# Scoring attention with unsplit float32 products of q and k, and theta with fp16 halves, in a fused attention and mixing kernel on one core

## The chip, the core and the metric

The kernel runs on one core of a Trainium2 chip. The metric is the device time of one execution in microseconds. Five engines work side by side, each through its own queue of instructions: PE (TensorE: PE is its matmuls, PEld its weight loads), DVE (VectorE), ACT (ScalarE), POOL (GpSimd) and SP, which here only issues transfers.

## The reference

Attention over 8 batches of 8 heads, 576 positions and 64 features, with a causal window of 128 and a linear bias, and then a mixing layer over the joined heads (512 channels):

```python
scores = scale * np.matmul(q, k.transpose(0, 1, 3, 2))
mask = (rel >= 0) & (rel < window)                      # window = 128
scores = np.where(mask, scores + bias[None], -1000000000.0)
attn = softmax(scores); attn_out = np.matmul(attn, v)
x = attn_out.transpose(0, 2, 1, 3).reshape(B, S, H * D)
theta = x @ w_theta
zr, zi = x * np.cos(theta), x * np.sin(theta)
y = np.einsum('ts,bsd->btd', w_tok_r, zr) + np.einsum('ts,bsd->btd', w_tok_i, zi)
u = x + y
return u + np.maximum(u @ w_ch, 0.0)
```

(softmax stands for the reference's maximum, exponential and normalization.) q, k and v are float32; the four weights of the mixing layer are float64.

## The kernel before

**Precision.** A product that must be better than one reduced pass is made of halves: an operand is split into a high part and the rest, and three products (high by high, rest by high, high by rest) are summed in PSUM. q and k, theta's x and w_theta, and u and w_ch are split into float32 halves of the type float32r; the weights P and v of the late heads, z and w_tok into fp16 halves.

**Stages.** Two heads form a pair `p`; 32 pairs, four to a batch.

- `load_pair` fetches q and k of a pair, transposed, each [128, 576] with one head on the upper 64 rows and the other on the lower. `split_pair` makes the halves: ACT casts qh (L395) and kh (L399), DVE subtracts ql (L396), and DVE (first eight pairs, two batches) or POOL (the others) subtracts kl (L329, a helper's line that also makes z_lo).
- `scores` goes through five tiles of up to 128 queries by 192 or 256 keys, in three groups ((0, 2), (3, 4), (1,)), all through one PSUM tile `s_ps` of two banks, a head in each. For each tile three products for two heads (L490). Then DVE adds the band (slope and mask) and takes the minimum (L506, two instructions each), and ACT takes the exponential (L511).
- The first seven pairs (`EARLY`) are turned on PE (L569) and multiplied by v in float32 (L579); the later ones are split into fp16 halves (ACT L525, DVE L527), turned by DMA and multiplied by v's halves (L597). DVE normalizes into `x_sb` (L542 to L546).
- `turn` is run once per batch: x is turned (PE L618), split (ACT L630, DVE L632) and copied (ACT L635), then theta for each of five row blocks (PE L650: 12 products of 512 columns, or 8 for the last 64 rows, which pack both halves of x into one operand). `w_theta` carries a factor 1/(2 pi), so the nearest integer is subtracted (ACT L664, DVE L665), and sine and cosine follow on ACT (L671, L673), z on DVE (L677) and its halves (ACT L682, L329).
- `mix` sums over positions (PE L713, 216 products of 288 columns a batch), `channels` over channels (PE L741, 96 products), and DVE adds (L719, L748).
- The float64 weights are unpacked into float32 on DVE and ACT (L338 to L376) at the start. For w_tok PE sums the magnitudes of columns (L348: products of ones with the exponents), and a power of two from their maximum (L780 to L790) scales the fp16 halves (L793, L796). w_theta's halves come straight from `whole` (L368, L370).

**Order.** Nothing is ordered by hand. `Plan` records every step with its buffers and a written cost, simulates the engines forward and backward six times, and emits the steps in the best order found. Where its plan leaves PE without work, `Plan.run` puts in fillers (`spin`, L297: products of ones into the unused end of an accumulator bank), which keep PE busy and compute nothing.

Of the kernel before, what the change touches and what calls it, by code (L numbers as in the profile page):

```python
# [13 lines left out]
F32 = mybir.dt.float32  # L14
# [84 lines left out]
class Step:  # L99
    __slots__ = ("n", "engine", "busy", "late", "emit", "deps", "after", "table", "port", "start")  # L100


class Plan:
# [5 lines left out]
    def add(self, engine, busy, late, emit, deps, table=None, port=False):  # L109
        s = Step()  # L110
        s.n, s.engine, s.emit, s.table, s.port = len(self.steps), engine, emit, table, port
        s.busy, s.late, s.deps, s.after = busy, late, deps, []
        for d in deps:
            self.steps[d].after.append(s.n)
        self.steps.append(s)
        return s

    def __call__(self, engine, cost, emit, r=(), w=(), table=None, port=None):
# [105 lines left out]
def attn_moe_kernel(ctx: ExitStack, tc: tile.TileContext, qt, kt, vx, wth, wtok, wch, band, out):  # L224
# [19 lines left out]
    peak, wscale, shrunk = fixed[:, 133:134], fixed[:, 134:135], fixed[:, 136:144]  # L244
    bands = place("bands", [128, H, 256], BF16)
    columns_at = [144]
# [9 lines left out]
    zs_ring = small(3, 3)  # L256
# [3 lines left out]
    wth_hi, wth_lo = place("wth_hi", [128, 4, DM], F32R), place("wth_lo", [128, 4, DM], F32R)  # L260
# [13 lines left out]
    qr_ring, kr_ring = ring("qr", 1, [128, S], F32), ring("kr", 1, [128, S], F32)  # L274
    qk_ring = Ring([tuple(place(n, [128, S], F32R) for n in ("qh", "ql", "kh", "kl"))])
# [10 lines left out]
    fg_ring = ring("fg", 2, [128, 2, 512], F32)  # L286
    xp_ring = ring("xp", 2, [128, 2, 512], F32R)
# [3 lines left out]
    spun = a_ring.tiles[1][:, NT * 65:]  # L291

    def spin(count):

        same = white.bitcast(BF16)
# [28 lines left out]
    held = [Buf(v) for v in values_at]  # L324

# [5 lines left out]
    def unpack(src, c, w, finish, last=False, first=False, summed=None, raw_buf=None):  # L331
# [13 lines left out]
        if summed:  # L345
            def add():
                for k in range(2):
                    nc.tensor.matmul(summed.tile[:, :HALF], white, ex.bitcast(F32)[:, k * HALF:(k + 1) * HALF],  # L348
# [10 lines left out]
    def whole(hi, lo, buf, scale):  # L359
        def finish(c, w, val, ex, E, M):  # L360
            plan("DVE", dve(w), lambda: nc.vector.tensor_tensor(out=val, in0=val, in1=ex, op=ALU.mult), r=[E], w=[M],
                 port=True)
            if scale is None:
                plan("ACT", act(w), lambda: nc.scalar.copy(hi[:, c, :], val), r=[M], w=[(buf, ("h", c))])
                less("POOL", w, lo[:, c, :], val, hi[:, c, :].bitcast(F32), r=[M, (buf, ("h", c))],
                     w=[(buf, ("l", c))])
            else:
                plan("ACT", act(w), lambda: nc.scalar.activation(hi[:, c, :], val, AF.Copy, scale=scale),  # L368
                     r=[M], w=[(buf, ("h", c))])
                plan("DVE", (0.61, 0.13), lambda: nc.vector.scalar_tensor_tensor(  # L370
                    out=lo[:, c, :], in0=val, scalar=scale, in1=hi[:, c, :].bitcast(F32), op0=ALU.mult,
                    op1=ALU.subtract), r=[M, (buf, ("h", c))], w=[(buf, ("l", c))], port=True)
        return finish

    def keep(c, w, val, ex, E, M):
        plan("DVE", dve(w), lambda: nc.vector.tensor_tensor(out=held[c].tile, in0=val, in1=ex, op=ALU.mult),  # L376
             r=[E, M], w=[(held[c], 0)], port=True)


    raw_qk, split_qk, group_v, group_scale = {}, {}, {}, {}  # L380
# [9 lines left out]

    def split_pair(p):
        qr, kr = raw_qk.pop(p)
        buf = qk_ring.take()
        qh, ql, kh, kl = buf.tile
        plan("ACT", act(S), lambda: nc.scalar.copy(qh, qr.tile), r=[(qr, 0)], w=[(buf, "qh")])  # L395
        plan("DVE", dve(S), lambda: nc.vector.tensor_tensor(  # L396
            out=ql, in0=qr.tile, in1=qh.bitcast(F32), op=ALU.subtract),
            r=[(qr, 0), (buf, "qh")], w=[(buf, "ql")], port=True)
        plan("ACT", act(S), lambda: nc.scalar.copy(kh, kr.tile), r=[(kr, 0)], w=[(buf, "kh")])  # L399
        less("POOL" if p >= QUICK * PAIRS_OF else "DVE", S, kl, kr.tile, kh.bitcast(F32),  # L400
             r=[(kr, 0), (buf, "kh")], w=[(buf, "kl")])
        split_qk[p] = buf
# [47 lines left out]
    def regain(b):  # L450
# [19 lines left out]
    def scores(p, weights):  # L470
        late = p >= EARLY
        qk = split_qk.pop(p)
        qh, ql, kh, kl = qk.tile
        terms = ((qh, kh), (ql, kh), (qh, kl))
        mx_buf = mx_ring.take()
        mx = mx_buf.tile.rearrange("p (e i) -> p e i", e=2)
        for tiles in GROUPS:
# [5 lines left out]
            def multiply(tiles=tiles, ps=ps, wide=wide):  # L483
                for k, i in enumerate(tiles):
                    q0, qn, k0, kn, _ = TILES[i]
                    kn = kn if wide else 256
                    for j, (qm, km) in enumerate(terms):
                        for e in range(2):
                            rows = slice(64 * e, 64 * e + 64)
                            nc.tensor.matmul(ps.tile[:qn, e, 256 * k:256 * k + kn], qm[rows, q0:q0 + qn],  # L490
                                             km[rows, k0:k0 + kn], start=(j == 0), stop=(j == 2))
            plan("PE", pe(360 * len(tiles) + 190), multiply, r=[(qk, x) for x in ("qh", "ql", "kh", "kl")],
                 w=[(ps, 0)])
# [109 lines left out]
    def turn(b, x_buf, zs):  # L603
        isx, ISX = zs.tile[:, 1:2], (zs, 1)
        xtf = xtf_ring.take()
# [3 lines left out]
        def columns(i):  # L609
# [12 lines left out]
            if i == 0:  # L622
                both = x_hi.rearrange("p (c a t) -> p c a t", a=2, t=64)
                plan("ACT", act(370), lambda: nc.scalar.activation(both[:, :, 0], src, AF.Copy, scale=isx),
                     r=[(x_ps, 0), ISX], w=[(xp, "h")])
                plan("DVE", (0.395, 0.13), lambda: nc.vector.scalar_tensor_tensor(
                    out=both[:, :, 1], in0=src, scalar=isx, in1=both[:, :, 0].bitcast(F32), op0=ALU.mult,
                    op1=ALU.subtract), r=[(x_ps, 0), (xp, "h"), ISX], w=[(xp, "l")])
            else:
                plan("ACT", act(600), lambda: nc.scalar.activation(x_hi, x_ps.tile, AF.Copy, scale=isx),  # L630
                     r=[(x_ps, 0), ISX], w=[(xp, "h")])
                plan("DVE", (0.66, 0.13), lambda: nc.vector.scalar_tensor_tensor(  # L632
                    out=x_lo, in0=x_ps.tile, scalar=isx, in1=x_hi.bitcast(F32), op0=ALU.mult, op1=ALU.subtract),
                    r=[(x_ps, 0), (xp, "h"), ISX], w=[(xp, "l")])
# [4 lines left out]
        def angle(i):  # L639
# [12 lines left out]
            plan("PE", pe(4 * len(prods) * (238 if i else 245)), multiply,  # L652
# [11 lines left out]
            plan("ACT", act(512), lambda: nc.scalar.activation(r[:n], th, AF.Copy, bias=MAGIC), r=[THK], w=[R])  # L664
# [215 lines left out]
```

## Time and profile before

| | |
|---|---|
| median of 3 runs | 688.94 us (686.01 to 689.36) |
| profiled execution | 687.63 us |
| its span, first to last instruction | 685.6 us |
| PE busy | 657.5 us (96%) |
| DVE, ACT, POOL busy | 576.1, 541.5, 198.7 us (84, 79, 29%) |
| fillers (L297) | 292, 33.3 us of PE |
| score products (L490) | 960 matmuls |
| theta products (L650) | 448 matmuls |

The span is the time from the first to the last instruction; the execution's own time is 2.0 us longer. Matmuls are pipelined and overlap in the trace, so the distance between the starts of two of them tells more than the length of one. Busy shares are averages over the whole span, and the stages differ: rows by stretch of time are needed beside them. A row of two or more instructions (x2) gives the time from the first start to the last end.

### The profile page before, as it was taken

To read this page: it belongs to the slowest core of one execution; us is meant where nothing else is said; L and a number is where in the kernel's file an instruction comes from. 1 tells how busy PE (TensorE), PEld (TensorE's weight loads), DVE (VectorE), ACT (ScalarE), POOL (GpSimd) and SP (SyncE) were. 2 spreads that over 40 slices of the span, in tenths; PEclk is the share of its full clock that TensorE was granted. 3 is DMA by queue.
4 is the path that set the end of the run, shared out by engine and by line. 5 is a ranking of instruction groups with operands and counts; after the bars stand their busy time and mean duration, and the time that the engine had idled before them with its cause. 6 is when DMAs were issued, how large, how long until landed. Compare 5 with 4: busy or idle time off the path is not lost.

```text
span 685.6 us, 15977 instructions
## 1 busy us (share of the span) xinstructions
PE 657.5 (96%) x6144; PEld 548.2 (80%) x6144; DVE 576.1 (84%) x1556; ACT 541.5 (79%) x975; POOL 198.7 (29%) x211
## 2 busy tenths in 40 slices
PE   7999988898999799999999999999999999999998
PEld 6787776786787677887788778987898879878877
DVE  7999999899899999999998988989979978636312
ACT  5866899946789989998999989888989998335310
POOL 0000002123411124633273335432623351315220
PEclk9999999999999999999999999999999999999999
DMA  9465212285756457657655774277465736000101
GB/s 335 161 194 178 66 35 74 59 187 131 133 116 139 123 108 162 139 141 143 144 121 141 138 165 88 80 176 151 100 130 116 122 59 115 27 1 27 44 1 70
DMA packets 147148, 79.52 MB, mean 116 GB/s; under 512 B 120192, under 2 KB 136576, under 8 KB 147072
## 3 DMA queue, kind: packets, MB, share of 16 engines
q1 hardware_dynamic: 147072, 78.50, 48.4%
q8 instruction: 48, 0.79, 0.5%
q14 instruction: 28, 0.23, 0.1%
HBM read 39.55 MB, written 9.44 MB: 71 GB/s over the span
## 4 chain that ended last, share of the span: by engine, by line
PE 40%; ACT 6%; DVE 3%; issue 1%; DVEq 0%; ACTq 0%
PE m_psb L713 9%; PE m_psa L713 8%; PE t_psb L650 7%; PE m_psb L741 5%; PE m_psa L741 4%; PE s_ps L490 3%; PE a_psb L597 1%; PE a_psa L597 1%; PE t_psa L650 1%; PE t_psa L618 1%; ACT L673 1%; DVE fgb L677 1%; ACT z_hi L682 1%; ACT L511 0%; ACT hlb L525 0%
## 5 line engine op out<-in xcount | busy, mean ns | idle before, releaser
L713 PEld LDWEIGHTS <-z_hi 128*128 128x128 f16 x1152 | 109.1, 99 | 36.5 <-issue 7.0
L713 PE MATMUL m_psb<-wtk_hi,z_hi 128*128 128x288 f16 x288 | 83.2, 289 | 2.9 <-DVE xtfa L719 2.5
L713 PE MATMUL m_psa<-wtk_hi,z_hi 128*128 128x288 f16 x288 | 83.3, 289 | 0.0
L713 PE MATMUL m_psa<-wtk_lo,z_hi 128*128 128x288 f16 x288 | 83.2, 289 | 0.0
L713 PE MATMUL m_psb<-wtk_hi,z_lo 128*128 128x288 f16 x288 | 83.1, 289 | 0.0
L713 PE MATMUL m_psa<-wtk_hi,z_lo 128*128 128x288 f16 x288 | 83.1, 289 | 0.0
L713 PE MATMUL m_psb<-wtk_lo,z_hi 128*128 128x288 f16 x288 | 83.0, 288 | 0.0
L713 PEld LDWEIGHTS <-z_lo 128*128 128x128 f16 x576 | 56.8, 99 | 15.1 <-DVE z_lo L329 0.3
L329 POOL TENSOR_TENSOR kl<-kra,kh 128x576 fp32r<-128x576 f32 x24 | 38.3, 1597 | 97.8 <-ACT kh L399 92.4
L490 PE MATMUL s_ps<-kh,qh 64*128 64x256 f32 (+1 forms) x320 | 53.4, 328 | 10.8 <-DVE fixed L506 9.9
L490 PEld LDWEIGHTS s_ps<-kh,qh 64*128 64x128 f32 (+1 forms) x320 | 28.6, 173 | 29.4 <-DVE fixed L506 13.2
L329 POOL TENSOR_TENSOR z_lo<-fgb,z_hi 128x512 f16<-128x512 f32 x27 | 35.7, 1337 | 42.6 <-ACT z_hi L682 22.9
L725 POOL TENSOR_TENSOR u_lo<-xtfb,u_hi 128x288 fp32r<-128x288 f32 x32 | 31.5, 994 | 56.4 <-ACT u_hi L723 54.5
L329 POOL TENSOR_TENSOR z_lo<-fga,z_hi 128x512 f16<-128x512 f32 x27 | 37.1, 1388 | 35.5 <-ACT z_hi L682 35.4
L490 PE MATMUL s_ps<-kh,ql 64*128 64x256 f32 (+1 forms) x320 | 44.7, 274 | 1.4 <-DVE ql L396 1.2
L725 POOL TENSOR_TENSOR u_lo<-xtfa,u_hi 128x288 fp32r<-128x288 f32 x32 | 30.3, 953 | 54.1 <-ACT u_hi L723 53.2
L490 PE MATMUL s_ps<-kl,qh 64*128 64x256 f32 (+1 forms) x320 | 44.4, 272 | 0.5 <-POOL kl L329 0.5
L511 ACT ACTIVATE sbb<-sbb,fixed 128x256 f32<-128x256 f32 (+1 forms) x84 | 36.5, 488 | 8.6 <-DVE fixed L506 8.4
L511 ACT ACTIVATE sba<-sba,fixed 128x256 f32<-128x256 f32 (+1 forms) x88 | 38.6, 489 | 5.1 <-DVE fixed L506 5.0
L673 ACT ACT_TABLE_LOAD x30 | 38.5, 1283 | 0.5
L511 ACT ACTIVATE sbc<-sbc,fixed 128x256 f32<-128x256 f32 (+1 forms) x84 | 36.0, 487 | 3.1 <-DVE fixed L506 3.0
L297 PE MATMUL a_psb<-white 128*128 128x187 bf16 x292 | 33.3, 272 | 5.1 <-DVE x_sbb L546 2.4
(315 smaller groups left out, 2016.0 us busy)
## 6 DMA issues: line engine op xcount, KB each, us to landing
kra<-in_kt_dram SPq DMA_DIRECT2D x32, 288.0 KB, 3.1
qra<-in_qt_dram SPq DMA_DIRECT2D x32, 288.0 KB, 3.3
out_dram<-xtfa SPq DMA_DIRECT2D x32, 144.0 KB, 2.0
out_dram<-xtfb SPq DMA_DIRECT2D x32, 144.0 KB, 1.8
vba<-in_vx_dram SPq DMA_DIRECT2D x6, 650.0 KB, 5.3
vbb<-in_vx_dram SPq DMA_DIRECT2D x5, 650.0 KB, 5.0
vbc<-in_vx_dram SPq DMA_DIRECT2D x5, 650.0 KB, 5.2
xtfb<-in_wch_dram SPq DMA_DIRECT2D x4, 512.0 KB, 4.8
```

Source lines behind the costliest of these rows:

```text
L297: nc.tensor.matmul(spun, same[:, :128], same[:, :spun.shape[-1]], start=True, stop=True)
L329: plan(engine, cost, lambda: on.tensor_tensor(out=out, in0=whole, in1=part, op=ALU.subtract), r=r, w=w, port=True)
L490: nc.tensor.matmul(ps.tile[:qn, e, 256 * k:256 * k + kn], qm[rows, q0:q0 + qn], km[rows, k0:k0 + kn], start=(j == 0), stop=(j == 2))
L511: plan("ACT", (0.187 + kn * 0.833e-3, 0.15), lambda part=part, least=least: nc.scalar.activation(part, part, AF.Exp, bias=least, scale=-1. ...
L597: nc.tensor.matmul(av[:, i, :r.shape[-1]], l, r, start=(j == 0), stop=(j == len(prods) - 1))
L618: nc.tensor.transpose(x_ps.tile[:, c * n:c * n + n], x_buf.tile[:n, i, c * 128:c * 128 + 128], ident[:n, :n])
L650: nc.tensor.matmul(t_ps, a[:, c * 128:c * 128 + 128], w[:, c, :], start=(k == 0 and c == 0), stop=(k == len(prods) - 1 and c == 3))
L673: plan("ACT", (0.53, 0.15), lambda: nc.scalar.activation(f[:n], f[:n], AF.Sin, scale=-RAD), w=[F], table="sin")
L677: plan("DVE", dve(512), lambda: nc.vector.tensor_tensor(out=dst, in0=x_buf.tile[:n, i, :], in1=src, op=ALU.mult), r=every + [key], w=[out_ ...
L713: nc.tensor.matmul(y.tile[:, :HALF], z[:, c, m * 128:m * 128 + 128], w[:, c, cs], start=(part == 0 and j == 0 and a == 0), stop=(part == 2 ...
L725: plan("POOL", pool(HALF), lambda m=m, cs=cs, at=at: nc.gpsimd.tensor_tensor(out=u_half("u_lo")[:, m, cs], in0=at, in1=u_half("u_hi")[:, m ...
L741: nc.tensor.matmul(o.tile[:, :HALF], w[:, c, e * 128:e * 128 + 128], u[:, c, cs], start=(k == 0), stop=(k == 11))
```

## The change

- `split_pair` is gone, with qh, ql, kh and kl. `scores` multiplies the loaded float32 q and k directly, one product for each head and tile instead of three (320 in place of 960). The raw q and k have three buffers each instead of one.
- theta's operands become fp16. w_theta is unpacked into `held_theta` (the float32 buffers that later hold sine and cosine), its column sums are taken on PE as w_tok's were, and `halve`, now shared by both weights, finds the power of two, scales and splits. x is split without the scale `isx`, so the scale of theta is carried by three columns for each batch (`unit`, `magic`, `rad`, four small DVE operations in `regain`): rounding adds `magic` in place of a constant, and sine and cosine take `rad` as scale.
- Fillers go to the accumulator bank that has rested longest, and are counted from when it rests; 168 of them are placed in place of 292.
- The written costs of the steps follow the edits, and the plan comes out in another order throughout.

```diff
-    def run(self, spin):
-        last = FIRST
+    def run(self, spin, tiles):
+        last, used = FIRST, [0.0] * len(tiles)
         for s in self.order():
             if s.engine == "PE":
-                spin(int(FILL * (s.start - last) / SPIN))
+                k = min(range(len(tiles)), key=lambda k: used[k])
+                spin(tiles[k], int(FILL * (s.start - max(last, used[k])) / SPIN))
                 last = s.start + s.busy
+            for k, t in enumerate(tiles):
+                if any(t is x for x in s.places):
+                    used[k] = s.start + s.busy + s.late
...
-    wth_hi, wth_lo = place("wth_hi", [128, 4, DM], F32R), place("wth_lo", [128, 4, DM], F32R)
+    wth_hi, wth_lo = place("wth_hi", [128, 4, DM], F16), place("wth_lo", [128, 4, DM], F16)
...
-    qr_ring, kr_ring = ring("qr", 1, [128, S], F32), ring("kr", 1, [128, S], F32)
-    qk_ring = Ring([tuple(place(n, [128, S], F32R) for n in ("qh", "ql", "kh", "kl"))])
+    qr_ring, kr_ring = ring("qr", 3, [128, S], F32), ring("kr", 3, [128, S], F32)
...
-    def split_pair(p):
...
-        plan("ACT", act(S), lambda: nc.scalar.copy(qh, qr.tile), r=[(qr, 0)], w=[(buf, "qh")])
-        plan("DVE", dve(S), lambda: nc.vector.tensor_tensor(
-            out=ql, in0=qr.tile, in1=qh.bitcast(F32), op=ALU.subtract),
...
-                    for j, (qm, km) in enumerate(terms):
-                        for e in range(2):
-                            rows = slice(64 * e, 64 * e + 64)
-                            nc.tensor.matmul(ps.tile[:qn, e, 256 * k:256 * k + kn], qm[rows, q0:q0 + qn],
-                                             km[rows, k0:k0 + kn], start=(j == 0), stop=(j == 2))
-            plan("PE", pe(360 * len(tiles) + 190), multiply, r=[(qk, x) for x in ("qh", "ql", "kh", "kl")],
+                    for e in range(2):
+                        rows = slice(64 * e, 64 * e + 64)
+                        nc.tensor.matmul(ps.tile[:qn, e, 256 * k:256 * k + kn], qr.tile[rows, q0:q0 + qn],
+                                         kr.tile[rows, k0:k0 + kn], start=True, stop=True)
+            plan("PE", pe(430 * len(tiles) + 100), multiply, r=[(qr, 0), (kr, 0)], w=[(ps, 0)])
...
+    def halve(held, sums, w, order, power, scale, factor, key, hi, lo, buf):
+        least = floor_of[key]
+        plan("DVE", dve(w // 2), lambda: nc.vector.tensor_reduce(
+            out=peak, in_=sums.tile[:, :w // 2], axis=mybir.AxisListType.X, op=ALU.max), r=[(sums, 0)],
+            w=[(ws_buf, "peak")])
...
+            plan("ACT", act(w), lambda c=c, val=val: nc.scalar.activation(hi[:, c, :], val, AF.Copy, scale=scale),
+                 r=[(held[c], 0), (ws_buf, key)], w=[(buf, ("h", c))])
+            plan("DVE", dve(w), lambda c=c, val=val: nc.vector.scalar_tensor_tensor(
+                out=lo[:, c, :], in0=val, scalar=scale, in1=hi[:, c, :], op0=ALU.mult, op1=ALU.subtract),
...
-                plan("ACT", act(600), lambda: nc.scalar.activation(x_hi, x_ps.tile, AF.Copy, scale=isx),
+                plan("ACT", act(600), lambda: nc.scalar.copy(x_hi, x_ps.tile), r=[(x_ps, 0)], w=[(xp, "h")])
...
-            plan("ACT", act(512), lambda: nc.scalar.activation(r[:n], th, AF.Copy, bias=MAGIC), r=[THK], w=[R])
+            plan("ACT", act(512), lambda: nc.scalar.activation(r[:n], th, AF.Identity, bias=magic[:n]),
...
+            plan("ACT", (0.53, 0.15), lambda: nc.scalar.activation(f[:n], f[:n], AF.Sin, scale=rad[:n]), r=[(zs, 5)],
...
     for c in range(4):
-        unpack(wth, c, DM, whole(wth_hi, wth_lo, theta_w, TURN))
+        unpack(wth, c, DM, keep(held_theta), first=c == 0, last=c == 3, summed=sums)
+    halve(held_theta, sums, DM, range(4), tscale, tturn, TURN, "t", wth_hi, wth_lo, theta_w)
```

Line numbers below are those of the kernel before, except in the rows of the order after, where the same work has other lines (scores L509 for L490, score evacuation L524 for L506, sums of weights L354 for L348, and so on).

On PE at the second pair, in its middle group of tiles, the rows before are these. `a_psa` and `a_psb` are outputs of heads of the first pair, the rest are score products:

```order
L579 MATMUL a_psa<-vba,pta 128x65 x9
L490 MATMUL s_ps<-kh,qh 128x256 x2
L490 MATMUL s_ps<-kh,ql 128x256 x2
L490 MATMUL s_ps<-kl,qh 128x256 x2
L490 MATMUL s_ps<-kh,qh 128x256 x2
L490 MATMUL s_ps<-kh,ql 128x256 x2
L490 MATMUL s_ps<-kl,qh 128x256 x2
L579 MATMUL a_psb<-vba,ptb 128x65 x9
```

After, on PE at the same pair (`krb`, `qrb` are its raw k and q, `krc`, `qrc` those of the third pair, `t_psa` takes the sums of w_theta):

```order
L587 MATMUL m_psa<-fixed,sbna 128x128
L509 MATMUL s_ps<-krb,qrb 128x256 x4
L597 MATMUL a_psa<-vba,pta 128x65 x9
L509 MATMUL s_ps<-krb,qrb 128x256 x2
L354 MATMUL t_psa<-u_lo,white 128x256 x2
L509 MATMUL s_ps<-krc,qrc 64x192 x2
L509 MATMUL s_ps<-krc,qrc 128x256 x2
```

The two-tile group has four products where it had twelve (first tile, head one and head two, then the second tile), and a chunk's sum of w_theta now stands between the scores of two pairs.

On DVE at the fourth pair, before, between the normalizing of two heads (`x_sba`):

```order
L545 RECIPROCAL fixed<-fixed 128x5
L546 TENSOR_TENSOR x_sba<-a_psa,fixed 128x5x64
L329 TENSOR_TENSOR kl<-kra,kh 128x576
L396 TENSOR_TENSOR ql<-qra,qh 128x576
L542 TENSOR_SCALAR fixed<-a_psb,fixed 128x5
```

After, on DVE where theta's power of two begins (the reduction L381 of the sums and the clamp L384), between score evacuation and the unpacking of weights:

```order
L524 ISA sba,fixed<-s_ps,bands 128x256
L524 ISA fixed 128x1
L360 SCALAR_TENSOR_TENSOR u_lo<-u_lo 128x576
L381 TENSOR_REDUCE fixed<-t_psa 128x1
L384 TENSOR_SCALAR fixed<-fixed 128x1
L357 SCALAR_TENSOR_TENSOR u_hi<-u_hi 128x512
L374 TENSOR_TENSOR fgb<-u_hi 128x512
```

The two 576-wide subtractions have left the queue, and narrow operations on sums and columns have come in.

On SP at the start of the program, before (`kra`, `qra` are the first pair's raw k and q, `xtfa`, `u_lo`, `u_hi` the places where w_theta is unpacked):

```order
L387 DMA kra<-in_kt_dram 128x576
L337 DMA xtfa<-in_wth_dram 128x1024
L337 DMA u_lo<-in_wth_dram 128x1024
L337 DMA u_hi<-in_wth_dram 128x1024
L385 DMA qra<-in_qt_dram 128x576
L316 DMA bands<-in_band_dram 128x2048
```

After, on SP at the start:

```order
L414 DMA kra<-in_kt_dram 128x576
L412 DMA qra<-in_qt_dram 128x576
L320 DMA bands<-in_band_dram 128x2048
L421 DMA vbb<-in_vx_dram 128x4x325
L421 DMA vba<-in_vx_dram 128x4x325
L414 DMA krb<-in_kt_dram 128x576
L412 DMA qrb<-in_qt_dram 128x576
L343 DMA u_hi<-in_wth_dram 128x1024
```

The bands have moved from sixth to third place, and w_theta from second to eighth.

More of the change, by code (lines that the diff above doesn't have):

```diff
@@ L99 @@
 class Step:
-    __slots__ = ("n", "engine", "busy", "late", "emit", "deps", "after", "table", "port", "start")
+    __slots__ = ("n", "engine", "busy", "late", "emit", "deps", "after", "table", "port", "start", "places")
 class Plan:
@@ L111, in add @@
         s.n, s.engine, s.emit, s.table, s.port = len(self.steps), engine, emit, table, port
-        s.busy, s.late, s.deps, s.after = busy, late, deps, []
+        s.busy, s.late, s.deps, s.after, s.places = busy, late, deps, [], ()
         for d in deps:
@@ L134, in __call__ @@
             s = self.add(engine, *cost, emit, deps, table, engine == "POOL" if port is None else port)
+        s.places = [buf.tile for buf, _ in r + w]
         for buf, region in r:
@@ L285, in attn_moe_kernel, with spin @@
     pt1_ring = ring("ptn", 2, [128, 4, 128], F16)
-    fg_ring = ring("fg", 2, [128, 2, 512], F32)
-    xp_ring = ring("xp", 2, [128, 2, 512], F32R)
+    fg_tiles = [place(f"fg{k}", [128, 2, 512], F32) for k in "ab"]
+    xp_ring = ring("xp", 2, [128, 2, 512], F16)
     s_ring = Ring([psum.tile([128, 2, 512], F32, name="s_ps")])
     a_ring, t_ring, m_ring = banks("a_ps", 2), banks("t_ps", 2), banks("m_ps", 2)
-    spun = a_ring.tiles[1][:, NT * 65:]
-    def spin(count):
-        same = white.bitcast(BF16)
+    def spin(tile, count):
+        spun, same = tile[:, NT * 65:], white.bitcast(BF16)
         for _ in range(count):
@@ L324, in attn_moe_kernel @@
     held = [Buf(v) for v in values_at]
+    held_theta = [Buf(t[:, k]) for t in fg_tiles for k in range(2)]
+    floor_of = {"t": 2.0 ** -20, "w": 2.0 ** -60}
     def less(engine, n, out, whole, part, r, w):
@@ L347, in add @@
                 for k in range(2):
-                    nc.tensor.matmul(summed.tile[:, :HALF], white, ex.bitcast(F32)[:, k * HALF:(k + 1) * HALF],
+                    nc.tensor.matmul(summed.tile[:, :w // 2], white, ex.bitcast(F32)[:, k * w // 2:(k + 1) * w // 2],
                                      start=first and k == 0, stop=last and k == 1)
@@ L375, in keep, with whole @@
[L375 to L380, printed above, removed]
+    def whole(c, w, val, ex, E, M):
+        plan("DVE", dve(w), lambda: nc.vector.tensor_tensor(out=val, in0=val, in1=ex, op=ALU.mult), r=[E], w=[M],
+             port=True)
+        plan("ACT", act(w), lambda: nc.scalar.copy(wch_hi[:, c, :], val), r=[M], w=[(chan_w, ("h", c))])
+        less("POOL", w, wch_lo[:, c, :], val, wch_hi[:, c, :].bitcast(F32), r=[M, (chan_w, ("h", c))],
+             w=[(chan_w, ("l", c))])
@@ L830, in attn_moe_kernel @@
     with tc.manual_schedule():
-        plan.run(spin)
+        plan.run(spin, a_ring.tiles)
 def _band():
```

121 lines of the change are left out of this document (54 added, 67 removed).

## The prediction

> **What bounds the kernel now.** I read the busy times first, then the busy times of two long stretches, the fillers in the same stretches, who made TensorE wait, and the end of the chain. In the windows view the columns are the busy time (and instruction count) of PE, PEld, DVE, ACT and POOL, then the granted clock, the DMA share and GB/s.
>
> ```profile
> PE 657.5 (96%) x6144; PEld 548.2 (80%) x6144; DVE 576.1 (84%) x1556; ACT 541.5 (79%) x975; POOL 198.7 (29%) x211
> ...
> 0.00:240.00 240.00, 215.65 (x1943) 179.17 (x1944) 223.42 (x641) 194.87 (x359) 34.62 (x50) 0.97 0.51 138
> 240.00:686.00 446.00, 441.85 (x4203) 368.99 (x4201) 352.68 (x916) 346.61 (x617) 164.11 (x161) 1.00 0.48 104
> ...
> 20.00:80.00 60.00, 57.91 (x454) 47.28 (x452) 58.88 (x182) 45.51 (x92) 0.99 (x5) 1.00 0.49 152
> 80.00:140.00 60.00, 51.18 (x445) 42.76 (x445) 56.16 (x162) 57.98 (x106) 7.07 (x9) 0.94 0.24 67
> 240.00:570.00 330.00, 329.56 (x3297) 272.10 (x3295) 302.73 (x819) 305.69 (x543) 133.39 (x131) 1.00 0.60 127
> ```
>
> The kernel has two regimes. From 240 us on PE is busy for 329.56 of 330 us, so a matmul more or less there is time more or less. Before 240 us DVE is the full engine (58.88 of 60, and 223.42 of 240), with ACT beside it from 80 to 140 (57.98 of 60). How little PE bounds that part is seen in its fillers (L297, products of ones that only keep it busy) and in its waits:
>
> ```profile
> 0.00:240.00 240.00, 33.32 (x292) 28.21 (x292) 0.97 0.51 138
> 240.00:686.00 446.00, 0.00 (x0) 0.00 (x0) 1.00 0.48 104
> ...
> PE s_ps L490 <- DVE fixed L506: 9.9, 10, 2.4
> ...
> 620.17 2.81 PE t_psb L650 x12
> 622.98 1.12 PE m_psb L713 x9
> ...
> 680.70 1.61 PE m_psa L741 x12
> ```
>
> All 292 fillers (first two rows: PE, then PEld) run before 240 us, 33.3 us of them; PE's longest wait is for DVE to empty the one score tile. The chain's rows show the end as PE alone. So the sum has two parts: what DVE is spared before 240 us, and what PE must do after it.
>
> **The change part by part.**
>
> *DVE before 240 us.* The low halves of q (L396), and of k for the first eight pairs (L329), go:
>
> ```profile
> 0.00:240.00 240.00, 12.20 (x15) 0.97 0.51 138
> ...
> L329 DVE TENSOR_TENSOR kl<-kra,kh 128x576 fp32r<-128x576 f32 x8 | 6.0, 752 | 2.8 <-ACT kh L399 2.8
> ...
> 20.01 0.75 DVE L329 TENSOR_TENSOR kl<-kra,kh 128x576 fp32r<-128x576 f32 x1
> 20.68 0.75 DVE L396 TENSOR_TENSOR ql<-qra,qh 128x576 fp32r<-128x576 f32 x1
> 21.35 0.27 DVE L427 TENSOR_REDUCE fixed<-t_psa 8x1 f32<-8x128 f32 x1
> ...
> 308.17 0.23 DVE L311 TENSOR_TENSOR fixed<-fixed 128x1 int32<-128x1 int32 x2
> ```
>
> Fifteen of L396 (first row) and eight of L329 stand there; one after the other they take 0.67 us of the queue each (20.01, 20.68, 21.35), so 23 x 0.67 = 15.4 us. Added for theta's power of two are one reduction (0.27 as L427) and five operations on one column (0.11 each, half of the L311 row), 0.8 us, and per batch four more such, 3 x 4 x 0.11 = 1.3 us. The product and the low half of each theta chunk stay one DVE operation each. Net 13.3 us less. In the order of DVE at the fourth pair, shown above, the two 576-wide subtractions are gone and what came is narrow.
>
> DVE is 93% busy in this part, so 0.93 x 13.3 = 12.4 us could reach the end. Against it, the first DVE work is now the evacuation of scores, which needs the bands:
>
> ```profile
> 4.48 0.76 DVE L329 TENSOR_TENSOR kl<-kra,kh 128x576 fp32r<-128x576 f32 x1 [2.80 <-ACT kh L399]
> ...
> 1.67 0.42 SPq L337 DMA_DIRECT2D u_lo<-in_wth_dram  x1
> ...
> bands<-in_band_dram SPq DMA_DIRECT2D x1, 512.0 KB, 6.8
> ```
>
> The bands are third in SP's queue now (issue near 1.67) instead of sixth; a landing 6.8 us after issue would be 8.5, and with less ahead of it I take 7, so DVE starts 2.5 us later than at 4.48. I take 12.4 - 2.5, about 10 us earlier. Bounds: 0 (ACT or order holds the part) and 16 us (all 15.4, rounded up). ACT would not hold it: it loses
>
> ```profile
> 0.00:240.00 240.00, 10.03 (x15) 0.97 0.51 138
> 0.00:240.00 240.00, 11.30 (x16) 0.97 0.51 138
> ...
> L671 ACT ACTIVATE fga<-fga,fixed 128x512 f32<-128x512 f32 x16 | 11.4, 710 | 0.0
> ...
> L673 ACT ACTIVATE fga<-fga 128x512 f32<-128x512 f32 x16 | 10.1, 631 | 1.4 <-DVE fga L668 1.2
> ```
>
> 21.3 us of casts (L395, L399) there. Column operands in place of constants cost it about 0.08 us each (710 against 631), on three activations of a theta tile, while x's high half loses one: 0.16 x 40 = 6.4 us over the whole run. After 240 us ACT and DVE have room (305.69 and 302.73 of 330), and so has POOL; what is taken off them there is hidden behind PE and counts nothing.
>
> *Scores on PE.* Rows of two matmuls are the two heads of a pair, on the upper and lower 64 rows:
>
> ```profile
> 418.92 0.29 PE L713 MATMUL m_psa<-wtk_hi,z_lo 128*128 128x288 f16 x1
> 419.13 0.39 PE L490 MATMUL s_ps<-kh,qh 64*128 64x256 f32 x2
> 419.36 0.28 PE L490 MATMUL s_ps<-kh,ql 64*128 64x256 f32 x2
> 419.47 0.28 PE L490 MATMUL s_ps<-kl,qh 64*128 64x256 f32 x2
> 419.68 1.20 PE L650 MATMUL t_psb<-wth_hi,xpa 128*128 128x512 f32 x4
> ...
> 54.15 1.14 PE L348 MATMUL t_psa<-xtfa,white 128*128 128x288 f32 x4
> 55.12 0.33 PE L297 MATMUL a_psb<-white 128*128 128x187 bf16 x2
> ...
> 240.00:686.00 446.00, 44.24 (x540) 33.19 (x540) 1.00 0.48 104
> ```
>
> Both heads run at once: two of 0.28 us last 0.28 together, and the next two follow 0.12 later (419.36, 419.47). A pair has four tiles of 256 columns and one of 192 (0.09 by width): 4 x 3 x 0.118 + 3 x 0.09 = 1.69 us now. The unsplit float32 product is seen at L348: a weight chunk is two products in the program and four matmul records here, four in 0.97 us, so two passes of 0.243 us for 288 columns, 1.68 ns a column. At 256 columns that is two passes of 0.216 (0.431), at 192 columns 0.32. If the two heads' passes run side by side as the split ones do, a pair costs 4 x 0.431 + 0.32 = 2.05 us, 0.36 more. The gaps around a group (0.2 us at 419.13 and at the first product) belong to the change between half and full rows and stay, since the groups stay. The 540 matmuls after 240 us are 18 pairs of 30: 18 x 0.36 = +6.5 us. That is the lower bound, as nothing shows a pass under the streaming rate. The upper: one head after the other, 2 x 2.05 = 4.10, +2.41 a pair, +43 us. I take the lower, as the nearest row for two 64-row products is these pairs.
>
> In the order of PE, shown above, twelve products of a two-tile group became four, head one's then head two's for each tile. Before 240 us the 14 other pairs add 5.0 us and the eight sums 8 x 0.431 = 3.4 us; 33.3 us of fillers and 24 us of idle PE cover that.
>
> *Theta on PE.* Single-pass float32 against fp16, at 512 columns:
>
> ```profile
> 420.71 1.10 PE L650 MATMUL t_psb<-wth_lo,xpa 128*128 128x512 f32 x4
> 421.65 1.10 PE L650 MATMUL t_psb<-wth_hi,xpa 128*128 128x512 f32 x4
> 422.59 0.69 PE L741 MATMUL m_psb<-u_hi,wch_hi 128*128 128x288 f32 x4
> ...
> 98.03 3.08 PE L297 MATMUL a_psb<-white 128*128 128x187 bf16 x36
> ...
> 418.80 0.29 PE L713 MATMUL m_psa<-wtk_lo,z_hi 128*128 128x288 f16 x1
> ...
> 240.00:686.00 446.00, 85.24 (x336) 61.32 (x336) 1.00 0.48 104
> ```
>
> Eight take 1.88 us (420.71 to 422.59), 0.235 each. Sixteen-bit products take 0.081 at 187 columns ((3.08 - 0.24)/35) and 0.122 at 288 (418.80 to 418.92), 0.41 ns a column more, so 0.215 to 0.217 at 512. Of 336 after 240 us each saves 0.018: -6.0 us. Bounds 0 and -6.7.
>
> *Fillers.* 168 instead of 292, on whichever accumulator tile rests longest; the later part had none. They cost nothing unless the clock falls (0.94 in 80 to 140 now).
>
> *Sum.* -10 + 6.5 - 6.0 = -9.5 us. The profiled execution took 687.63 us (span 685.6 and 2.0 around it), so 678.1; the median of the runs, 688.94, lies 1.3 above it, and I say 679.
>
> **The rivals.**
>
> B, *the heads fall out of step, and it ends slower.* The rows show the two heads abreast where they alternate, one matmul each. An unsplit product is two passes, and in the order above head one's both come first. If passes start in program order, head one's second waits for its first on the same rows, and head two's first stands behind it; each group then lasts one pass of 0.216 us longer. Three groups a pair: 0.65 us, so +1.01 a pair, 18.2 us after 240, and about 2 us leak through before. -10 + 18.2 - 6.0 + 2 = +4, 692 us. The change turns slower where a pair costs 0.36 + 9.5/18 = 0.89 us more. [...]
>
> C, *the heads run one after the other.* +43 - 6, and the early part's gain is eaten by 14 x 2.41 = 34 us more on PE against 57 us of cover that isn't evenly spread: 724 to 732. Against it speak the L490 rows; for it, that none of them is a two-pass product.
>
> D, *the early gain doesn't come.* ACT (57.98 of 60 from 80 to 140) and the wait for the one score tile (9.9 us) set that part, and the 10 us shrink to 0 to 2: 0 to -2 + 6.5 - 6.0, 686 to 688, no change. Against it, ACT loses more than DVE does there.
>
> **How the numbers follow.** A (the forecast) 0.46, B 0.26, C 0.11, D 0.17. A measurement tells about 0.5%, 3.4 us. A gives faster but for 0.02; B is slower in 0.17, same in 0.07, faster in 0.02; D is same in 0.12, faster in 0.05. Faster 0.51, same 0.21, slower 0.28. Range: below 16 - 0.5 us under the profile (671); above to B with more leaking through (697); outside it C and some 0.08. A's own range is 671 to 685.
>
> **What would show it.** From the first matmul of a one-tile score group to the product after it are 0.55 us now (419.13 to 419.68). A makes it 0.55 + 0.43 - 0.35 = 0.63 us, B 0.84, C 1.06; that row decides most. Theta's twelve products in 2.6 us instead of 2.81 confirm their term. A first unbroken, fillerless stretch of PE from about 230 us shows the early gain; one from 240 us again, with DVE still full before it, shows D. If the clock fell under 0.94 between 80 and 140 us, the fillers were missed. What would make me wrong is mostly the pace of two-pass products on 64 rows, which no row shows.

## The result and the profile after

The changed kernel takes 670.5 us (median of four runs, 667.8 to 673.1), the kernel before 689.15 us beside it: 0.9736 of the time, 95% interval 0.9676 to 0.9797. The profiled execution took 668.13 us, its span 666.3. The median lies 0.5 us under the range given, 8.5 us under the forecast.

The busy times of the whole span, and then two windows (columns as above):

```profile
PE 647.6 (97%) x5716; PEld 486.3 (73%) x5716; DVE 533.5 (80%) x1553; ACT 506.3 (76%) x907; POOL 154.4 (23%) x187
...
0.00:240.00 240.00, 224.75 (x1881) 165.88 (x1881) 225.01 (x686) 190.26 (x359) 26.33 (x49) 1.00 0.58 155
240.00:667.00 427.00, 422.82 (x3836) 320.46 (x3835) 308.48 (x868) 316.03 (x549) 128.07 (x138) 1.00 0.44 99
```

PE works more in the first 240 us (224.75 against 215.65) though 124 fillers are gone, and DVE is as full as before: the part that DVE sets has become shorter, not looser. The granted clock is 1.00 where it was 0.97.

The same windows for the fillers, the score products and theta's products alone (PE, then PEld):

```profile
0.00:240.00 240.00, 18.40 (x168) 14.94 (x168) 1.00 0.58 155
...
240.00:667.00 427.00, 50.24 (x332) 25.09 (x332) 1.00 0.44 99
...
240.00:667.00 427.00, 71.90 (x312) 29.11 (x312) 1.00 0.44 99
```

A pair now has 20 score matmuls (each product is two passes), so 332 are 16.6 pairs where 18 were left before. What made PE wait longest, and the first work of DVE:

```profile
PE s_ps L509 <- DVE fixed L524: 6.1, 9, 1.3
PE t_psb L637 <- DVE xpb L649: 3.4, 2, 2.6
...
8.38 0.35 DVE L524 CUSTOM_DVE_ANT_0 sba<-s_ps,bands 64x192 f32<-64x192 f32 x1 [6.71 <-DMA bands<-in_band_dram]
```

The wait for the one score tile shrank from 9.9 to 6.1 us. DVE begins at 8.38 us instead of 4.48, since the bands land then.

The rows that the prediction asked for: a one-tile score group, the two-tile groups of tiles (0, 2) and (3, 4), each with the product after it, and theta:

```profile
399.88 0.29 PE L730 MATMUL m_psa<-wtk_hi,z_lo 128*128 128x288 f16 x1
400.10 0.70 PE L509 MATMUL s_ps<-krc,qrc 64*128 64x256 f32 x4
400.74 0.30 PE L730 MATMUL m_psb<-wtk_hi,z_hi 128*128 128x288 f16 x1
...
257.22 1.18 PE L509 MATMUL s_ps<-krb,qrb 64*64 64x192 f32 x8
258.32 0.30 PE L730 MATMUL m_psa<-wtk_hi,z_hi 128*128 128x288 f16 x1
...
411.85 1.14 PE L509 MATMUL s_ps<-kra,qra 64*128 64x256 f32 x8
412.92 0.20 PE L615 MATMUL a_psb<-vhb,pta 128*128 128x65 f16 x1
...
405.84 1.04 PE L666 MATMUL t_psa<-wth_hi,xpb 128*128 128x512 f16 x4
406.71 1.03 PE L666 MATMUL t_psa<-wth_lo,xpb 128*128 128x512 f16 x4
```

The one-tile group takes 0.64 us to the next product: A said 0.63, B 0.84, C 1.06. Four theta products take 0.87 us (406.71 - 405.84), 0.2175 each, where the prediction had 0.217.

Where the time went is seen when each PE matmul is given the time up to the start of the next, and the trace is cut at the last filler (231.9 us before, 219.5 after). I worked these sums out from the start times of the two profiled executions:

| us | before | changed |
|---|---|---|
| ahead of the last filler: products | 179.8 | 187.3 |
| ahead of it: fillers and idle | 53.6 | 31.3 |
| behind it: scores | 41.0 (18.2 pairs) | 49.7 (17.6 pairs) |
| behind it: theta (336 products) | 81.0 | 71.8 |
| behind it: all else | 325.5 | 321.5 |

The first part contains 18 products of the position sum (18 x 0.122 = 2.2 us) and 0.6 score pairs (1.7 us) more than before, 3.9 us moved out of the second part. So the first part became 233.4 - 218.6 + 3.9 = 18.7 us shorter, and the second 447.5 - 443.0 - 3.9 = 0.6 us. The prediction had 10 us shorter for the first and 0.5 us longer for the second (+6.5 - 6.0).

### The profile page after: what moved, and what is told of

Read it like the earlier page. It is cut to its first block, busy times and chain, and to the rows that moved or that the text cites. A ratio compares the mean times of both kernels' runs of the same rounds, so it can differ in the third digit from the quotient of the medians.

```text
span 666.3 us, 14953 instructions
## 1 busy us (share of the span) xinstructions
PE 647.6 (97%) x5716; PEld 486.3 (73%) x5716; DVE 533.5 (80%) x1553; ACT 506.3 (76%) x907; POOL 154.4 (23%) x187
## 4 chain that ended last, share of the span: by engine, by line
PE 62%; DVE 4%; ACT 4%; issue 1%; DVEq 0%; ACTq 0%
PE m_psb L730 13%; PE m_psa L730 13%; PE t_psa L666 9%; PE s_ps L509 7%; PE m_psb L758 6%; PE m_psa L758 6%; PE a_psb L615 2%; PE a_psa L615 2%; PE t_psb L637 1%; PE t_psb L666 1%; DVE fgb L694 0%; ACT sba L529 0%; ACT L529 0%; ACT L690 0%; DVE sbc L524 0%
## 5 line engine op out<-in xcount | busy, mean ns | idle before, releaser
L335 POOL TENSOR_TENSOR z_lo<-fga,z_hi 128x512 f16<-128x512 f32 x27 | 34.3, 1277 | 49.3 <-ACT z_hi L699 37.2
L335 POOL TENSOR_TENSOR z_lo<-fgb,z_hi 128x512 f16<-128x512 f32 x27 | 34.1, 1276 | 41.1 <-ACT z_hi L699 40.6
L666 PEld LDWEIGHTS <-xpb 128*128 128x128 f16 x224 | 21.3, 98 | 24.8 <-issue 1.8
L666 PEld LDWEIGHTS <-xpa 128*128 128x128 f16 x224 | 20.8, 98 | 24.5 <-issue 1.7
L524 DVE CUSTOM_DVE_ANT_0 sba<-s_ps,bands 128x256 f32<-128x256 f32 (+1 forms) x88 | 30.5, 395 | 9.6 <-DMA bands<-in_band_dram 6.7
L509 PE MATMUL s_ps<-kra,qra 64*128 64x256 f32 (+1 forms) x220 | 34.1, 410 | 2.7 <-DVE fixed L524 1.8
L509 PE MATMUL s_ps<-krb,qrb 64*128 64x256 f32 (+1 forms) x220 | 33.3, 401 | 2.6 <-DVE fixed L524 2.4
```

The costliest lines, as they stand in the source:

```text
L335: plan(engine, cost, lambda: on.tensor_tensor(out=out, in0=whole, in1=part, op=ALU.subtract), r=r, w=w, port=True)
L509: nc.tensor.matmul(ps.tile[:qn, e, 256 * k:256 * k + kn], qr.tile[rows, q0:q0 + qn], kr.tile[rows, k0:k0 + kn], start=True, stop=True)
L524: kn=kn, c0=c0: nc.vector.tensor_tensor_reduce(out=part, in0=ps.tile[:qn, e, 256 * k:256 * k + kn], in1=bands[:qn, (2 * p + e) % H, c0:c0 ...
L666: nc.tensor.matmul(t_ps, a[:, c * 128:c * 128 + 128], w[:, c, :], start=(k == 0 and c == 0), stop=(k == len(prods) - 1 and c == 3))
```

## Which edit brings it

**The score edit alone.** q and k unsplit, three raw buffers, and nothing else:

```diff
-    qk_ring = Ring([tuple(place(n, [128, S], F32R) for n in ("qh", "ql", "kh", "kl"))])
-        split_pair(p)
-    terms = ((qh, kh), (ql, kh), (qh, kl))
+    qr.tile[rows, q0:q0 + qn], kr.tile[rows, k0:k0 + kn], start=True, stop=True
```

> The score edit alone: unsplit float32 products, no halves of q and k, three raw buffers; theta stays in float32 halves, and the fillers are placed by the old rule (157 of them by the new plan). E (the early part is worth more than 10 us): PE after 240 us pays +6 us for the pairs left there, and the early part gives 16 us or more, so 10 us faster than before, about 679 us. F (most of the gain is theta's and the fillers'): the early part gives the 10 us of the prediction and the scores take 6.5 back, so 3 to 4 us faster, about 685.

676.7 us, 0.9799 of before (0.9762 to 0.9835): about 13.5 us, more than E. With the 6.5 us that the prediction lets the scores take back, the early part would give about 20 us. Some 4 of the 13.5 go with a higher granted clock (a median of 0.9935 against 0.983), as the section on the clock works out.

**Theta alone.**

```diff
-    wth_hi, wth_lo = place("wth_hi", [128, 4, DM], F32R), place("wth_lo", [128, 4, DM], F32R)
+    wth_hi, wth_lo = place("wth_hi", [128, 4, DM], F16), place("wth_lo", [128, 4, DM], F16)
+    halve(held_theta, sums, DM, range(4), tscale, tturn, TURN, "t", wth_hi, wth_lo, theta_w)
```

> Theta with fp16 halves alone; scores stay split, old filler rule (341 fillers by the plan). E: 336 products after 240 us, each 0.018 us (prediction) to 0.026 us (start to start in the changed kernel) cheaper, 6 to 9 us faster, 680 to 683; the early part gets 2 us more work on DVE for the sums, so 682. F: the same edit also frees the early part (no scaled copies), 12 us or more, 677 or less.

685.94 us, 0.994 (0.9918 to 0.9962): 4.2 us, less than E and far from F. Its later part, in the windows view:

```profile
240.00:570.00 330.00, 326.57 (x3322) 251.83 (x3320) 303.74 (x844) 312.09 (x553) 134.05 (x134) 1.00 0.61 127
```

PE has 3.4 us of holes there where it had 0.4 before (329.56 of 330), with ACT at 312.09: cheaper products turn partly into waiting. The column sums of w_theta add 5.4 us of PE time besides, by the same start times.

**The fillers' rule alone.**

```diff
-                spin(int(FILL * (s.start - last) / SPIN))
+                k = min(range(len(tiles)), key=lambda k: used[k])
+                spin(tiles[k], int(FILL * (s.start - max(last, used[k])) / SPIN))
```

> Only the fillers' rule changed: they go to the accumulator bank that has rested longest and are counted from there (279 instead of 292). E: the fillers cost nothing, within 1 us of before. F: fillers that waited for DVE held PE up, and the clock rests at half for four stretches of 3.4 us; without that 4 to 7 us faster, about 683.

688.34 us, 0.9979 (0.9951 to 1.0006): no change that can be told from nothing. F, which had 4 to 7 us, falls.

**Scores and theta, old fillers' rule.** The same two edits together.

> The changed kernel with the old filler rule (170 fillers, on one bank, by the plan). E: same as the changed kernel within 2 us, 670 to 673. F: 4 to 7 us slower than the changed kernel, 675 to 678, with half-clock stretches in the profile.

671.03 us, 0.9731 (0.9692 to 0.9771): all of the gain is there without the new rule, as E had it.

## What the early part was freed of

These start from the changed kernel and put one thing back. The first four shared a chip on which before took 692.58 us. The changed kernel itself was run again on another chip, beside the fifth of them (the same work later) and two of the versions further below:

> The changed kernel itself, unedited, beside the others of this chip: 0.9736 of before's time. Every theory expects 0.970 to 0.978, about 671 us where before takes 690.

670.05 us beside 691.35, 0.9708 (0.9676 to 0.974). The pieces below are differences of ratios to this one, times 690 us. Each ratio has an interval of about 0.0035 to either side, 2.4 us, and the runs differ in their granted clock, so the section on the clock gives the pieces once more at equal clock.

**DVE's work.**

```diff
+    rest = Buf(place("rest", [128, S], F32R))
+        for _ in range((p < 15) + (p < 8)):
+            plan("DVE", dve(S), lambda: nc.vector.tensor_tensor(
+                out=rest.tile, in0=qr.tile, in1=kr.tile, op=ALU.subtract), r=[(qr, 0), (kr, 0)], w=[(rest, 0)], port=True)
```

> The changed kernel (670.5 us) with the 23 subtractions of 576 columns put back on DVE as idle work: two for each of the first eight pairs, one for each of the next seven, into a scratch tile that nobody reads. W (the early part is DVE's work): 23 x 0.67 = 15.4 us of queue, times DVE's 0.93 busy share, 12 to 15 us slower, about 684. L (what went is the chain load, cast, subtract, product, in which PE waited): DVE has room once nobody waits for it, 2 to 5 us slower, about 674.

682.36 us, 0.9852 (0.9815 to 0.989): 0.0144 above the changed kernel, 9.9 us. In its trace the idle subtractions (first row, DVE alone) and all engines in the first 240 us:

```profile
0.00:240.00 240.00, 16.22 (x22) 0.99 0.52 144
...
0.00:240.00 240.00, 225.62 (x1881) 166.75 (x1881) 227.67 (x679) 182.21 (x340) 20.23 (x43) 0.99 0.52 144
```

Of 16.22 us of added work on a queue that is 95% busy some 10 come out at the end, between W and L and nearer to W. At equal clock it is 12.3 us (section on the clock), which is W.

**ACT's work.** The casts in place of the subtractions:

```diff
+        for src in (qr, kr) if p < 15 else ():
+            plan("ACT", act(S), lambda src=src: nc.scalar.copy(cast.tile, src.tile), r=[(src, 0)], w=[(cast, 0)])
```

> The changed kernel with the 30 casts of 576 columns (q and k of the first 15 pairs) put back on ACT as idle work that nobody reads. W: ACT is not the bound, within 2 us of 670.5. ACT theory (ACT holds the early part, 57.98 of 60 us from 80 to 140 before): 20 us of ACT work, 8 us or more slower, about 679 or more.

674.04 us, 0.9728 (0.9691 to 0.9765): within 1.4 us of the changed kernel. ACT carries it:

```profile
0.00:240.00 240.00, 227.99 (x1855) 167.04 (x1855) 222.92 (x683) 207.80 (x385) 23.48 (x46) 0.98 0.55 150
```

ACT is 17.5 us busier there than in the changed kernel (207.80 against 190.26). By the ratios that costs nothing that can be told, at equal clock 2.6 us. Either is far from the 8 us or more of the ACT theory, so rival D's reason, that ACT holds the early part, is out.

**Both, and the scores wait for them.**

```diff
-multiply, r=[(qr, 0), (kr, 0)], w=[(ps, 0)])
+multiply, r=[(qr, 0), (kr, 0)] + extra, w=[(ps, 0)])
```

> Both sets of idle work put back, and the scores of a pair wait for its casts and subtractions, as they did before; products stay unsplit, three raw buffers stay. W: as the DVE work alone, 12 to 15 us slower, about 684. L: the whole of the early gain is given back, 16 us or more slower, about 687, where DVE work alone gives back 2 to 5.

687.41 us (684.51 to 690.13), 0.9921 (0.9888 to 0.9954): 4.8 us above the work on DVE alone on the same chip, and the ranges of the two don't meet. L's total (about 687) is met, but not its share, since DVE's work alone already gives back 9.9 us. The other 4.8 are not the price of the dependence alone. This run also has the casts on ACT, which by themselves cost 1.4 us (2.6 at equal clock), and its median clock is lower (0.992 against 0.9945); at equal clock 3.2 us are left for the casts and the dependence together. No run puts back the dependence without the casts, and no single wait shows it, so its own price stays open. What is still left to before, 5.4 us, goes with the clock: a median of 0.992 against 0.980, which by the line below is worth 4.9 us.

**One raw buffer.**

```diff
-    qr_ring, kr_ring = ring("qr", 3, [128, S], F32), ring("kr", 3, [128, S], F32)
+    qr_ring, kr_ring = ring("qr", 1, [128, S], F32), ring("kr", 1, [128, S], F32)
```

> The changed kernel with one raw buffer each for q and k, as before: a pair's load waits until the scores of the pair ahead are done. W: a load takes about 3 us and a pair's turn on DVE more than 10 in the early part, within 2 us of 670.5. L: the loads stand in the chain, 5 us or more slower, 676 or more.

677.91 us, 0.9785 (0.9747 to 0.9822): 5.3 us above the changed kernel, as L had it, and 9.8 at equal clock, since its runs are at 0.997 to 1.000. SP's queue shows loads of k that wait for the scores of the pair ahead, here and then in the changed kernel:

```profile
SPq L414 <- PE s_ps L509: 105.8, 24, 12.7
...
SPq L414 <- PE s_ps L509: 48.4, 11, 10.0
```

Before the change the halves had buffers of their own, so a raw buffer was free as soon as its pair was split. Without the split, the two more raw buffers are needed to keep that.

**The same work on DVE, later.** Two subtractions for each of pairs 17 to 24 and one for each of 25 to 31:

```diff
-        for _ in range((p < 15) + (p < 8)):
+        for _ in range((p >= 17) + (17 <= p < 25)):
```

> The same 23 idle subtractions on DVE as in the run with DVE work, but two for each of the 17th to 24th further pairs and one for each of the next, all after 240 us, where PE is the bound. W: hidden, within 2 us of the changed kernel. L or any theory in which DVE bounds the whole run: 10 us or more slower.

672.52 us, 0.9722 (0.9689 to 0.9754), at equal granted clock (0.987) 673.4 us as the changed kernel itself (673.4 and 673.6). The work is hidden there, as W had it.

## What the clock brings

The 20 runs of before in the first comparison have mean granted clocks from 0.975 to 0.992, and their times follow: 692.4 us in the mean of the two lowest, 685.1 at the highest; a straight line through all gives 4.1 us for each 0.01. The changed kernel's own four runs are 667.8 and 668.1 us at 1.000 and 672.9 and 673.1 at 0.987 and 0.989.

One hole of PE shows where two executions of one program part. Windows of the changed kernel's two profiled executions, the first of 666.3 us and the repeated one of 669.2:

```profile
120.00:126.00 6.00, 3.68 (x37) 3.44 (x38) 5.17 (x16) 5.97 (x11) 1.27 (x1) 1.00 0.30 87
126.00:137.00 11.00, 10.86 (x93) 9.75 (x93) 10.72 (x30) 6.87 (x14) 2.10 (x4) 1.00 0.70 106
...
120.00:126.00 6.00, 3.62 (x35) 3.19 (x34) 5.55 (x16) 5.97 (x10) 1.26 (x1) 1.00 0.28 82
126.00:137.00 11.00, 11.00 (x54) 9.59 (x55) 8.09 (x23) 4.62 (x11) 1.04 (x3) 0.53 0.59 109
```

Both have the same hole (PE 3.68 and 3.62 of 6 us). In the second the clock then falls to half for 10.24 us, and PE gets through 54 matmuls instead of 93. The half-clock stretches in all traces here are multiples of 3.41 us (apart from one at the very end of each), and in the 3.41 us ahead of 28 of the 34 PE was busy for less than half. In the trace of before there are four of one such length, from 85.60, 129.97, 157.28 and 235.78 us; PE was busy for 77% of the 3.41 us ahead of the first and for 0.98, 0.95 and 1.24 us of those ahead of the others. The stretch of 10.24 us is not among the 28: it begins at 126.43 us, 2.9 us behind the end of the hole, and PE was busy for 83% of the 3.41 us ahead of it. In three other traces, too, the clock falls 2.1 to 2.9 us behind this hole. Why the same hole of 2.3 us goes with half the clock in one execution and not in the other, no run shows.

**No fillers.**

```diff
-FILL = 0.6
+FILL = 0.0
```

> The changed kernel without any filler; nothing else changes. Q (fillers keep the clock up and cost nothing): the granted clock falls from 0.99-1.00 to 0.98 or lower, at 4.2 us for each 0.01 some 5 to 10 us slower, 676 to 681. R (fillers only take PE's time): 0 to 5 us faster, and the clock stays.

678.15 us, 0.9814 (0.9786 to 0.9842), 7.3 us above the changed kernel, as Q had it. The median clock is 0.977 against 0.9945, and from 80 to 140 us it is down to 0.82:

```profile
80.00:140.00 60.00, 47.23 (x264) 32.52 (x262) 55.14 (x150) 52.52 (x97) 4.88 (x8) 0.82 0.23 65
```

**More fillers, in the kernel before and in the changed one.**

```diff
-FILL = 0.6
+FILL = 0.9
```

> The kernel before, with fillers put into 0.9 of each planned hole of PE instead of 0.6 (442 instead of 292); nothing else. Q (the clock's loss is about 5 us of the difference between the kernels): the clock rises from 0.98 to 0.99 or more, 3 to 6 us faster than before, 684 to 687. R (the clock is a sign of the holes, not a cost): the clock rises, the time stays within 1.5 us, or grows where fillers stand in the way.

688.42 us, 0.9953 (0.9929 to 0.9977): 3.2 us faster, clocks 0.985 to 0.997. That speaks for Q: the clock is a cost, not only a sign of the holes. Its median rose from 0.980 to 0.988, less than Q had, and by the line above that gives 3.3 us.

> The changed kernel with 0.9 in place of 0.6 (257 fillers instead of 168). Q: the granted clock stays at 1.00 in all runs, the median falls to the runs at full clock, 667 to 668.5. R: as the changed kernel, 670 to 672, or slower, since fillers stand in front of products.

671.23 us, 0.971 (0.9675 to 0.9745), as the changed kernel: two runs at 1.000 (667.0 and 667.4), four at 0.990 to 0.992 (671 to 673). So Q fails here. In the profiled run, one at 1.000, PE's wait for DVE in the hole at 122 us is down to 1.43 us from 2.32, with 30 fillers ahead of it in place of 20: the plan knows the hole, but the real one is longer. Where the four others lost the clock no kept trace shows.

At equal clock the two kernels can now be compared on one chip: at 0.987 before took 687.8 and 688.3 us, the changed kernel 673.4 and 673.6. So 14.5 us are the change's own, and 4 to 7 us, by the comparison, go with the higher clock.

The pieces of the last section can be read in the same way. A line through the ten runs of the changed kernel (667.7 us at 1.000, 4.35 us more for each 0.01 less) has none of them more than 0.7 us off it. The table gives how far other runs lie above that line at their own clock, in the mean. These are estimates, as they take the slope to hold for all the versions.

| version | us above the line |
|---|---|
| before (17 runs at 0.984 or more) | 15.0 |
| scores alone | 5.6 |
| theta alone | 13.2 |
| DVE's work | 12.3 |
| ACT's work | 2.6 |
| both, and the scores wait | 15.5 |
| one raw buffer | 9.8 |
| the same work on DVE, later | 0.1 |

At equal clock the score edit alone is thus worth 9.4 us and theta alone 1.8, and the work and the waiting of the split, put back together, cost as much as the whole change gains.

## Versions that might beat both

**The split kept where PE is full.** Unsplit for the first 15 pairs, split for the others:

```diff
+        if p >= 15:
+            split_pair(p)
```

> Unsplit products for the first 15 pairs, where DVE is full, and the old split into float32 halves for the other 17 (casts on ACT, the low half of q on DVE, of k on POOL), where PE is full. P (PE's own work sets the later part): a pair's scores cost PE 2.25 us split and 2.82 unsplit, start to start, so 17 x 0.57 = 9.7 us faster than the changed kernel, about 661. N (the split's work on ACT, DVE and POOL or its chain takes it back): within 3 us of the changed kernel, 668 to 673.

671.64 us, 0.9722 (0.9696 to 0.9748), as N had it. PE's scores fell by 9.1 us (90.3 to 81.2, start to start), and the time did not (by the line above, at equal clock, it is 0.8 us under the changed kernel). The wait that took it, and the windows around it:

```profile
PE s_ps L529 <- DVE fixed L544: 2.7, 1, 2.7
...
300.00:318.00 18.00, 18.00 (x190) 13.59 (x189) 17.76 (x38) 16.72 (x27) 4.01 (x5) 1.00 0.83 164
318.00:336.00 18.00, 15.30 (x138) 10.25 (x137) 17.00 (x47) 13.44 (x27) 6.58 (x8) 0.81 0.56 97
```

With the split back DVE is full here (17.76 and 17.00 of 18), the score tile is emptied late, PE stands for 2.7 us, and the clock falls to half for 6.83 us behind it. Fillers and idle grew by 5.5 us in all; the rest went into slower products of the position sum (2.0 us) and others.

**The same for the last 12 pairs only** (`if p >= 20`).

> The split into float32 halves kept for the last 12 pairs alone (from about 300 us on), unsplit products for the first 20. P: 12 x 0.57 = 6.8 us faster than the changed kernel, 663 to 665, since DVE is at 0.85 of the time from 330 to 570 us. N: a hole on PE opens as in the run with 17 pairs (2.7 us and half clock behind it), and it is within 2 us of the changed kernel.

672.88 us, 0.9722 (0.9686 to 0.9758), N again: scores fell by 7.0 us, and fillers and idle grew by 5.6.

```profile
240.00:570.00 330.00, 325.54 (x3224) 248.32 (x3222) 296.72 (x814) 299.88 (x526) 129.91 (x129) 1.00 0.58 123
...
PE s_ps L529 <- DVE fixed L544: 3.4, 3, 2.0
```

What PE saves comes back as holes (4.5 us in this window, 0.2 in the changed kernel's): DVE and ACT are at 0.9 there, and 3.4 of the 4.5 us are waits for DVE to empty the one score tile.

**The bands in two transfers**, two heads first:

```diff
-    plan("SP", (0.4, 1.6, 1.9), lambda: nc.sync.dma_start(out=bands, in_=band), w=[(band_buf, 0)])
+    for part, cost in ((slice(0, 2), (0.4, 0.5, 1.9)), (slice(2, H), (0.4, 1.2, 1.9))):
```

> The changed kernel with the bands' transfer cut in two: 128 KB for the first two heads in third place, 384 KB for the others behind the second pair's q and k. If the wait for the bands (6.71 us on DVE, ending at 8.38) is paid in full, DVE starts some 1.2 us sooner (384 KB at about 320 GB/s) and the kernel is 1 to 2 us faster, about 669; if ACT's or PE's work or the order eats it, no change that can be told.

673.77 us, 0.9745 (0.9715 to 0.9775): not faster. DVE does start 1.9 us sooner, but now waits for PE:

```profile
6.50 0.35 DVE L526 CUSTOM_DVE_ANT_0 sba<-s_ps,bands 64x192 f32<-64x192 f32 x1 [4.83 <-PE s_ps L511]
...
4.39 2.06 PE L511 MATMUL s_ps<-kra,qra 64*64 64x192 f32 x8 [0.74 <-DMA qra<-in_qt_dram]
```

What the later bands cost the changed kernel therefore stays open. No version here beats the changed kernel.

## Why the prediction was right and wrong

**Right.** The scores of two heads run abreast (A). In the group at 257.22 the passes of the first tile start in twos, at 257.217 and 257.224, then at 257.431 and 257.438. The rows don't name the head; two starts 0.007 us apart, where a pass takes 0.21, are read here as the two heads side by side. By that reading the passes alternate between the heads, and B's error was to take a product's two passes as neighbours. Theta's products went from 0.235 to 0.2175 us. After 240 us the two terms nearly cancel, as said.

**Mis-sized, but cancelling, which is luck.** Scores cost +0.57 us a pair behind the last filler (49.7/17.6 against 41.0/18.2), not 0.36. By the medians from a group's first product to the next other one, the one-tile group grew by 0.085 us (0.550 to 0.635) and the group of tiles 3 and 4 by 0.161 (0.905 to 1.066), near the 0.08 and 0.15 of the prediction's rates. The group of tiles 0 and 2 grew by 0.317 (0.790 to 1.107), where the rates give 0.13. Its weight loads:

```profile
257.22 0.19 PEld L509 LDWEIGHTS s_ps<-krb,qrb 64*64 64x64 f32 x4 [0.24 <-DVE hlb L545]
257.69 0.30 PEld L509 LDWEIGHTS s_ps<-krb,qrb 64*128 64x128 f32 x4 [0.28 <-issue]
```

Tile 0 has 64 queries, tile 2 has 128 (64*64 and 64*128 in the rows). The loads of the second shape begin at 257.69 only, with no wait shown. Start to start the passes take 0.214, 0.259, 0.320 and 0.314 us in this group, and 0.320, 0.216, 0.216 and 0.314 in the one of tiles 3 and 4. So the first and the last pass of a group are long in both, and here the two beside the change of shape as well: 0.259 where 192 columns at the prediction's rate take 0.16, and 0.320 where 256 take 0.216. The prediction took the gaps around a group to stay and had no price for a change of shape within it. Theta gave -9.2 us behind the last filler instead of -6.0: the mean distance of two of its starts fell from 0.240 to 0.216 us, since some 20 of 307 before stood 0.33 apart, and the distance from a block's last product to the next other one fell from 0.248 to 0.187 (means of 29). Together +0.8 instead of +0.5 us.

**Wrong: the early gain of 10 us.** It was 18.7 in the profiled pair. Two steps failed. First, the sum counted DVE's queue time alone as what the early part is spared, and put ACT's casts and the waiting of the scores for their halves at nothing. At equal clock the subtractions put back as work cost 12.3 us, where 0.93 x 15.4 gives 14.3; with the casts and the dependence on top it was 15.5. The 3.2 us between stood at nothing in the sum, and how they divide stays open. Second, the fillers and the clock: "they cost nothing unless the clock falls" looked only downward. The clock was under 1.00 before (0.97 in the first 240 us, four half-clock stretches of 3.41 us), and fillers and idle on PE fell from 53.6 to 31.3 us, so it could rise; 0.010 of clock is 4.1 us in the profiled pair.

10 - 2.0 + 3.2 + 4.1 make 15.3 of the 18.7. The other 3.4 us stay open: the sum had taken off 1.9 for the new narrow work and 2.5 for the bands, and no run shows what either cost at the end, though DVE did start 3.9 us later. With the clock's gain in the sum the forecast would have been about 675, and the range's low end about 667. How far under the range the median fell is in part chance: two of the four runs of the changed kernel kept the full clock (667.8 and 668.1 us), and the other two lie inside the range (672.9 and 673.1).

That the fillers' new rule does nothing by itself was right in effect (688.34), and ACT did not hold the early part.

## What to carry to other kernels

Count the work taken off a full engine at no more than its queue time (here 12.3 of 16.2 us came out); what others lose by waiting for it is to be added (3.2 us here, for the casts and the wait together), and a run that puts back the wait alone is needed to price it. Where the granted clock is under 1.00 in the stage that a change loosens (0.97 in the first 240 us here, 1.00 after), count the clock as a gain to be had, and compare runs at equal clock before giving the difference to the edit. Cheaper products in a stage where DVE and ACT ran at 0.9 came back as holes here: scores 7.0 us less in the last 12 pairs, fillers and idle 5.6 more.

## What the runs showed that was not expected

Unsplit float32 products on 64 rows run two heads abreast, 0.216 us a pass of 256 columns within a group, but the first and last pass of a group of such tiles take 0.32 us, and the two passes beside a change from 64 to 128 columns of weights within a group take some 0.1 us more each than by their columns (0.259 where 192 columns take 0.16, 0.320 where 256 take 0.216; the same in the medians of 17 such groups). What happens in PE at such a change no run shows. A hole of 2.3 us on PE left the clock alone in one execution and halved it for 10.24 us in another (span 666.3 and 669.2). The mean clock of an execution goes with most of the spread of one program here: 4.1 us for each 0.01 in 20 runs of before, 4.35 in ten of the changed kernel.
